# Turning the x operands of two token blocks by transposing DMAs instead of TensorE transposes and ScalarE copies

## The chip, the core and the metric

The kernel runs on one core of one Trainium2 chip. The metric is the device time of one execution in microseconds. The engines are TensorE (PE; its weight loads are PEld), VectorE (DVE), ScalarE (ACT), GpSimd (POOL) and SyncE (SP), whose queue issues most DMAs, in order; all DMAs run on 16 DMA engines.

## What is computed

`u` has 2048 tokens of 512 features. It is normalised (`xn`), and three terms are summed: `u` itself, a long convolution with a state-space kernel, and a mixture of eight experts in which all eight are used (top 8 of 8), so each token goes through every expert:

```
xn = layernorm(u)
out = u + s4_conv(xn) + xn * Dskip + sum_e gate[:, e] * (silu(xn @ w1[e]) @ w2[e])
# w1: 8 x 512 x 1792, w2: 8 x 1792 x 512, gate = softmax(xn @ w_gate)
```

The kernel keeps float32 accuracy with float16 matmuls: each operand is split into a high and a low half, and a product is three matmuls (high x high, high x low, low x high).

## The kernel before, in words

The experts run one after another (loop `e`), each over four blocks of 512 tokens (loop `tb`). The first product of an expert, `xn @ w1`, is done by a seven-product scheme on 2x2 blocks (Strassen-Winograd): instead of four quarters of x it takes seven sums and differences of them. For a token block `g` these operands are needed with features on partitions, in high and low halves. They lie in DRAM in `xd[g]` and are loaded from there into the single SBUF tile `xop`, seven pieces of 256 KB, at the end of the block before (lines 1562 to 1566, in `block`): each piece as soon as the last product that reads the old piece has been issued.

The operands are made once, while the first expert runs. Block 0 is handled by a separate path. Block 1 is turned straight into `xop`. Blocks 2 and 3 are made for `xd` in halves `(g, a)`, by these steps:

- `x_sums` (line 230): VectorE forms the seven sums, and SP stores the plain x to DRAM (lines 246 to 248, tensor `xnd`).
- `x_high` (line 251): ScalarE casts them to the high half, tile `xh`, one buffer. `x_low` (line 257): VectorE makes the low half, tile `xl`, one buffer.
- `x_turn` (line 264), four times for a half, `q` = 0 to 3 (0 and 1 the high half, 2 and 3 the low one): eight or six TensorE transposes of 128x128 into the shared PSUM bank `tp`, a ScalarE copy to the tile `xs` in SBUF (line 287), and two DMAs by SP to `xd` (line 291).

The order of all work is written out by hand. Time is counted in slots; 16 slots make a token block, four of them (one call of `block`) a group of expert columns. In a slot the products of `xn @ w1` are issued first, with ScalarE's work on them (`activate`, line 1355, which writes the tiles `ahl`); then the functions put into `mid`; then `pop` issues matmuls of the second product, which read `ahl` tiles of earlier slots; then the functions put into `side` and the pieces of work on the next expert's weights, which a planner admits by ScalarE time left (`act_room`, `work_on`). `early` stands before the products, `copied` behind the first of them. The registrations of the steps above are at lines 1466 to 1485: half `n` begins in slot `s0 = 20 + 4 n`, so the third block (`g` = 2, used from slot 32) is made in slots 20 to 27 and the fourth (used from slot 48) in slots 28 to 37.

The tiles `xs` and `ahl` share the nine buffers of the tag `hh`. The PSUM bank of `tp` is shared with other small products; `take_bank`, `bank_free` and the set `turns` keep their users apart: `turns` holds slots in which a step of the totals for a weight scale (`piece_end`, line 546) may not begin its bank use.

Of the kernel before, what the change touches and what calls it, by code (L numbers as in the profile page):

```python
# [10 lines left out]
F16 = mybir.dt.float16  # L11
# [7 lines left out]
P = 128  # L19
# [14 lines left out]
def s4_moe_kernel(  # L34
# [15 lines left out]
    nc = tc.nc  # L50
    V, S, T = nc.vector, nc.scalar, nc.tensor
# [17 lines left out]
    sb = ctx.enter_context(tc.tile_pool(name="sb", bufs=2))  # L69
# [13 lines left out]
    xop = cp.tile([P, 7, 2, 2, TH], F16, name="xop")  # L83
# [7 lines left out]
    xd = [dr.tile([P, 7, 2, 2, TH], F16, name=f"xd{g}") for g in range(NB)]  # L91
# [9 lines left out]
    clock = {"slot": 0, "pe": 0.0, "pe0": 0.0, "dve": 0.0, "dve0": 0.0, "left": 0.0,  # L101
             "act": 0.0, "act0": 0.0, "pe1": 0.0, "actleft": 0.0, "two": False}
    bank = {"out": None, "at": -1}

    def take_bank(out=None):

        f, bank["out"] = bank["out"], None
        if f:
            f()
            bank["at"] = clock["slot"]  # L110
        bank["out"] = out

    def bank_free():


        if bank["out"]:
            if clock["two"]:
                return False
            take_bank()
        return clock["slot"] > bank["at"]  # L120
# [104 lines left out]
    xs_ = {}  # L225
# [4 lines left out]
    def x_sums(g, a):  # L230


        ut, rs8 = uts[g], xs_["rs8", g]
        i0, i1 = g * TPB + a, g * TPB + a + 2
        m0, m1, r0, r1 = mean[:, i0:i0 + 1], mean[:, i1:i1 + 1], rs8[:, a:a + 1], rs8[:, a + 2:a + 3]
        fa_ = sb.tile([P, 4, TH], F32, tag="k4", name=f"xfa{g}_{a}", bufs=1)
        fb_ = sb.tile([P, 3, TH], F32, tag="v3", name=f"xfb{g}_{a}", bufs=1)
        a21 = sb.tile([P, TH], F32, tag="z", name=f"a21{g}_{a}", bufs=1)
        V.tensor_scalar(fa_[:, 0:2, :].rearrange("p a d -> p (a d)"), ut[a], m0, r0, op0=ALU.subtract, op1=ALU.mult)
        V.tensor_scalar(a21, ut[a + 2][:, 0:TH], m1, r1, op0=ALU.subtract, op1=ALU.mult)  # L240
        V.tensor_scalar(fa_[:, 2, :], ut[a + 2][:, TH:], m1, r1, op0=ALU.subtract, op1=ALU.mult)
        V.tensor_tensor(fa_[:, 3, :], a21, fa_[:, 2, :], op=ALU.add)
        V.tensor_tensor(fb_[:, 0, :], fa_[:, 3, :], fa_[:, 0, :], op=ALU.subtract)
        V.tensor_tensor(fb_[:, 1, :], a21, fa_[:, 0, :], op=ALU.subtract)
        V.tensor_tensor(fb_[:, 2, :], fa_[:, 1, :], fb_[:, 0, :], op=ALU.subtract)
        nc.sync.dma_start(xnd[:, i0, :], fa_[:, 0:2, :].rearrange("p a d -> p (a d)"))
        nc.sync.dma_start(xnd[:, i1, 0:TH], a21)
        nc.sync.dma_start(xnd[:, i1, TH:], fa_[:, 2, :])
        xs_["f"] = ((fa_, 0, 4), (fb_, 4, 3))

    def x_high(g, a):
        hi = xs_["hi"] = sb.tile([P, 7, TH], F16, tag="ta", name=f"xh{g}_{a}", bufs=1)
        for src, n0, n in xs_["f"]:
            S.copy(hi[:, n0:n0 + n, :].rearrange("p o d -> p (o d)"), src.rearrange("p o d -> p (o d)"))
            clock["act"] += at_(n * TH)

    def x_low(g, a):
        hi = xs_["hi"]
        lo = xs_["lo"] = sb.tile([P, 7, TH], F16, tag="tt", name=f"xl{g}_{a}", bufs=1)
        for src, n0, n in xs_["f"]:  # L260
            V.tensor_tensor(lo[:, n0:n0 + n, :].rearrange("p o d -> p (o d)"), src.rearrange("p o d -> p (o d)"),
                            hi[:, n0:n0 + n, :].rearrange("p o d -> p (o d)"), op=ALU.subtract)

    def x_turn(g, a, q):


        hi, lo = xs_["hi"], xs_["lo"]
        if g == 1:
            parts = [(r // 4, r // 2 % 2, r % 2) for r in range(8 * q, min(8 * q + 8, 28))]
        else:  # L270
            b, o0 = q // 2, q % 2 * 4
            no = min(4, 7 - o0)
            parts = [(o0 + r // 2, b, r % 2) for r in range(2 * no)]
        n = len(parts)
        take_bank()
        tp = ps_s.tile([P, 8, P], F16, tag="s4", name=f"tp{g}_{a}_{q}")
        for r, (o, b, k) in enumerate(parts):
            T.transpose(tp[:, r, :], (hi, lo)[b][:, o, k * P:(k + 1) * P], ident)  # L278
        if g == 1:
            dst = xop.rearrange("p o a k t -> p (o a k) t")[:, 8 * q:8 * q + n, a * P:(a + 1) * P]  # L280
            if q % 2:
                V.tensor_copy(dst, tp[:, :n, :])
            else:
                S.copy(dst, tp[:, :n, :])
        else:
            xs = sb.tile([P, 4, 2, P], F16, tag="hh", name=f"xs{g}_{a}_{q}", bufs=9)
            S.copy(xs.rearrange("p o k t -> p (o k) t")[:, :n], tp[:, :n, :])
            clock["act"] += at_(n * P)
            bank["at"] = now()
            for k in range(2):  # L290
                nc.sync.dma_start(xd[g][:, o0:o0 + no, b, k, a * P:(a + 1) * P], xs[:, :no, k])

    def x0_send(n):

# [10 lines left out]
    def x0_load():  # L305
        xs_["x0"] = sb.tile([P, 2, KT, TB], F16, tag="tb", name="x0", bufs=1)
        nc.sync.dma_start(xs_["x0"], x0d)
# [141 lines left out]
    def prepass_end(e, w, n):  # L449
        r = sb.tile([P, 1], F32, tag="r2", name=f"r2_{e}_{w}")  # L450
        V.tensor_reduce(r, rows[e, w][:, :n], axis=AX.X, op=ALU.add)
        yield
        st = pow2_total(r, 1, f"w{e}_{w}")
        yield
        if bank["out"]:
            take_bank()
        if w == 0:
            sc = scales[e] = sb.tile([P, 5], F32, tag="sc", name=f"sc{e}", bufs=2)
            w1_scales(sc, st, f"w{e}")
        else:  # L460
            sc = scales[e]
            pow2_scale(sc[:, 1:2], st, f"v{e}")
            pow2_inverse(sc[:, 4:5], sc[:, 1:2])
            V.scalar_tensor_tensor(sc[:, 4:5], sc[:, 4:5], float(2.0 ** (XSH - 1 + ASH)), sc[:, 2:3], op0=ALU.mult, op1=ALU.mult)
            ge_ = sb.tile([P, NT], F32, tag="gse", name=f"gse{e}", bufs=2)
            gates_e[e] = ge_
            if e > 1:
                V.tensor_scalar(ge_, gate[:, :, e], sc[:, 4:5], None, op0=ALU.mult)
# [77 lines left out]
    def piece_end(e, w, n, ready):  # L546

        st = {"g": prepass_end(e, w, n)}

        def step(k):  # L550
            st["at"] = now()
            next(st["g"], None)
            done.add((e, w, k))
            clock["dve"] += (0.2, 0.0, 0.9)[k]

        def can_go():
            if "at" not in st:
                return ready()
            return now() > st["at"] + 1 and bank_free() and now() + 1 not in turns
        it = Item(None, [lambda raw, k=k: step(k) for k in range(3)], can_go)  # L560
        it.e, it.w, it.sums = e, w, False
        return [it]
# [349 lines left out]
    def at_(n):  # L912

        return n / 1050 + 0.17
# [10 lines left out]
    def now():  # L925
        return clock["slot"]
# [174 lines left out]
    for pr in range(3, NPR):  # L1101
        for h in range(2):
            n = 2 * (pr - 3) + h
            tag, bufs = ("sE", 1) if n == 0 else ("sCB", 3) if n < 4 else ("stg", 4)
            t = sb.tile([P, D], F32, tag=tag, name=f"f0_{pr}_{h}", bufs=bufs)
# [9 lines left out]
    for pr in range(NPR):  # L1115
        t = w2s[pr].rearrange("p a f d -> p (a f d)").bitcast(F32)
# [289 lines left out]
        lows.append((first_split(2), True, False, None))  # L1406
    early, mid, copied = {}, {}, {}

    turns = set()

    def at(n, f, where=side):
        where.setdefault((0, n // 16, n % 16 // 4, n % 4), []).append(f)
    for n in range(7):
# [53 lines left out]
    for n, (g, a) in enumerate(halves):  # L1467
        s0 = 20 + 4 * n
        at(s0, lambda g=g, a=a: x_high(g, a), copied if n == 0 else side)
        at(s0 + 1, lambda g=g, a=a: x_low(g, a))  # L1470
        for q in range(4):
            n1, where = s0 + 2 + q, mid
            if (g, a) == (2, 1):
                n1, where = ((26, early), (26, mid), (27, early), (27, mid))[q]
            elif (g, a) == (2, 0) and q > 1:
                n1, where = 24, (early, mid)[q - 2]
            at(n1, lambda g=g, a=a, q=q: x_turn(g, a, q), where)
            turns.add(n1 - 2)
        if a == 0:
            at(s0 + 3, lambda g=g: x_sums(g, 1))  # L1480
            at(s0 + 3, lambda g=g: load_x(g + 1) if g + 1 < NB else x0_load())
        elif g + 1 < NB:
            at(s0 + 1, lambda g=g: norm_sums(g + 1))
            at(s0 + 2, lambda g=g: x_stats(g + 1))
            at(s0 + 3, lambda g=g: x_sums(g + 1, 0))
# [42 lines left out]
    for i in range(NT):  # L1528
        n = (i + 2) // 3
# [184 lines left out]
```

## Time and profile before

| what | value |
| --- | --- |
| timed runs (3) | 2329.56, 2329.60, 2330.28 us; median 2329.6 |
| span of the profiled execution | 2329.1 us |
| TensorE busy | 2315.5 us, 99% of the span |
| VectorE, ScalarE, GpSimd busy | 84%, 63%, 15% of the span |
| granted TensorE clock | 1.000 over the span |
| DMA | 320.72 MB in 327686 packets, 138 GB/s on average |

The span runs from the first to the last instruction of one execution; no other time of that execution is given, and the median of the timed runs is 0.5 us longer. In the rows below, `x8` behind a row is a count of instructions that the view has merged, `SPq` is an issue on SP's queue, and "to landing" runs from the issue of a DMA to its completion.

### The profile page before, as it was taken

To read this page: it belongs to the slowest core of one execution; us is meant where nothing else is said; L and a number is where in the kernel's file an instruction comes from. 1 tells how busy PE (TensorE), PEld (TensorE's weight loads), DVE (VectorE), ACT (ScalarE), POOL (GpSimd) and SP (SyncE) were. 2 spreads that over 40 slices of the span, in tenths; PEclk is the share of its full clock that TensorE was granted. 3 is DMA by queue.
4 is the path that set the end of the run, shared out by engine and by line. 5 is a ranking of instruction groups with operands and counts; after the bars stand their busy time and mean duration, and the time that the engine had idled before them with its cause. 6 is when DMAs were issued, how large, how long until landed. Compare 5 with 4: busy or idle time off the path is not lost.

```text
span 2329.1 us, 45278 instructions
## 1 busy us (share of the span) xinstructions
PE 2315.5 (99%) x17713; PEld 1540.1 (66%) x17713; DVE 1964.7 (84%) x3816; ACT 1466.2 (63%) x2585; POOL 339.7 (15%) x394
## 2 busy tenths in 40 slices
PE   8999999999999999999999999999999999999999
PEld 4666666666666666666666666666666666666665
DVE  8864877999999999999899989999989987997721
ACT  7676666657666576665766657666566665764543
POOL 0000011121111211111111111111111110111112
PEclk9999999999999999999999999999999999999999
DMA  8597456665566755655556545565465663643447
GB/s 281 181 264 199 111 137 151 146 146 118 133 160 144 149 129 130 155 117 107 131 121 161 117 102 139 125 148 123 99 144 123 145 133 86 154 94 65 81 87 176
DMA packets 327686, 320.72 MB, mean 138 GB/s; under 512 B 183664, under 2 KB 220016, under 8 KB 327024
## 3 DMA queue, kind: packets, MB, share of 16 engines
q1 hardware_dynamic: 271024, 223.70, 32.5%
q0 software_dynamic: 55872, 93.61, 25.5%
q8 instruction: 138, 2.26, 0.4%
q14 instruction: 76, 0.62, 0.1%
q10 hardware_dynamic: 576, 0.52, 0.1%
HBM read 202.14 MB, written 66.06 MB: 115 GB/s over the span
## 4 chain that ended last, share of the span: by engine, by line
PE 98%; ACT 1%; DVE 1%; DMA 0%; issue 0%; SPq 0%; DVEq 0%; ACTq 0%
PE hb L1348 43%; PE y L1333 16%; PE y L1331 16%; PE y L1332 16%; PE hb L1623 2%; PE kgen L769 1%; PE yp L900 1%; PE kf L840 1%; PE uf L827 1%; PE tp L278 0%; DMA xop<-xd 0%; DMA ut0b<-in_u_dram 0%; DMA kd<-ksb 0%; ACT ahl L1368 0%; ACT ye L1306 0%
## 5 line engine op out<-in xcount | busy, mean ns | idle before, releaser
L1348 PE MATMUL hb<-xop,w1s 128*128 128x256 f16 x9114 | 1072.6, 273 | 0.7 <-ACT scC L1570 0.4
L1348 PEld LDWEIGHTS <-w1s 128*128 128x128 f16 x9114 | 885.2, 98 | 174.1 <-issue 1.9
L1333 PE MATMUL y<-w2s,ahl 128*128 128x512 f16 x1792 | 679.2, 379 | 0.0
L1332 PE MATMUL y<-w2s,ahl 128*128 128x512 f16 x1792 | 679.2, 379 | 0.0
L1331 PE MATMUL y<-w2s,ahl 128*128 128x512 f16 x1792 | 679.2, 379 | 0.0
L1333 PEld LDWEIGHTS <-ahl 128*128 128x128 f16 x1792 | 175.4, 98 | 211.4
L1541 POOL DMA_DIRECT2D scC<-sE x124 | 120.3, 970 | 1282.9 <-ACT sE L1570 1050.6
L1364 ACT ACTIVATE fa<-hb,sc 128x512 f32<-128x512 f32 (+1 forms) x252 | 160.6, 637 | 200.5 <-PE hb L1348 196.6
L872 DVE TENSOR_TENSOR s<-s,tm 128x720 f32<-128x720 f32 (+14 forms) x480 | 268.9, 560 | 16.6
L1332 PEld LDWEIGHTS <-ahl 128*128 128x128 f16 x1792 | 175.4, 98 | 161.3
L1331 PEld LDWEIGHTS <-ahl 128*128 128x128 f16 x1792 | 175.4, 98 | 161.1
L871 DVE TENSOR_TENSOR tm<-v,k 128x720 f32<-128x720 f32 (+14 forms) x480 | 267.4, 557 | 10.6
L1377 DVE SCALAR_TENSOR_TENSOR ahl<-fa,sc,ahl 128x512 f16<-128x512 f32 (+1 forms) x262 | 178.6, 682 | 60.9 <-ACT ahl L1368 60.4
L1585 ACT COPY hb<-hb 128x512 f32<-128x512 f32 x124 | 64.1, 517 | 231.9 <-PE hb L1348 231.7
L1368 ACT ACTIVATE ahl<-fa,sc 128x512 f16<-128x512 f32 (+1 forms) x262 | 175.8, 672 | 8.5
L1541 POOL DMA_DIRECT2D scB<-sE x124 | 107.0, 863 | 428.9 <-ACT scB L1570 291.9
L1575 ACT COPY hb<-hb 128x512 f32<-128x512 f32 x124 | 64.3, 519 | 164.0 <-PE hb L1348 163.4
L1377 DVE SCALAR_TENSOR_TENSOR ahl<-scB,sc,ahl 128x512 f16<-128x512 f32 x124 | 84.4, 680 | 78.6 <-ACT ahl L1368 76.3
L757 DVE TENSOR_TENSOR tb<-ta,tt 128x64 f32<-128x64 f32 (+2 forms) x192 | 131.9, 687 | 5.6
L751 DVE TENSOR_TENSOR ta<-tb,zr 128x64 f32<-128x64 f32 (+2 forms) x192 | 131.6, 685 | 5.2
L1377 DVE SCALAR_TENSOR_TENSOR ahl<-scC,sc,ahl 128x512 f16<-128x512 f32 x124 | 84.2, 679 | 59.7 <-ACT ahl L1368 55.0
L1309 POOL DMA_DIRECT2D oacc<-ye x108 | 96.2, 1343 | 248.1 <-ACT ye L1306 246.4
(247 smaller groups left out, 2451.0 us busy)
## 6 DMA issues: line engine op xcount, KB each, us to landing
xop<-xd SPq DMA_DIRECT2D x210, 256.0 KB, 3.9
pp<-in_w_dram SPq DMA_DIRECT2D x98, 512.0 KB, 4.0
raw<-in_w_dram SPq DMA_DIRECT2D x56, 512.0 KB, 5.4
oacc<-ye POOLq DMA_DIRECT2D x108, 256.0 KB, 6.4
scC<-sE POOLq DMA_DIRECT2D x93, 256.0 KB, 4.2
scB<-sE POOLq DMA_DIRECT2D x93, 256.0 KB, 4.1
raw<-in_w_dram SPq DMA_DIRECT2D x52, 256.0 KB, 4.0
raw<-in_w_dram SPq DMA_DIRECT2D x104, 128.0 KB, 4.0
```

The source lines that it names most:

```text
L751: V.tensor_tensor(ta, tin, zrv, op=ALU.mult)
L757: V.tensor_tensor(tout, ta, tt, op=ALU.add)
L871: V.tensor_tensor(tm, v3f[:, :, 0:n], kb, op=ALU.mult)
L872: V.tensor_tensor(s3[:, :, m:], s3[:, :, m:], tm, op=ALU.add)
L1331: T.matmul(y, lhs[0], w2s[pr][:, 0, fh, :], start=(c == 0), stop=False)
L1332: T.matmul(y, lhs[0], w2s[pr][:, 1, fh, :], start=False, stop=False)
L1333: T.matmul(y, lhs[1], w2s[pr][:, 0, fh, :], start=False, stop=(c == NF - 1))
L1348: T.matmul(dst[:, q, :], w1s[pr][:, a, wo, k * P:(k + 1) * P], xop[:, xo, b, k, :], start=(first_mm and q == 0 and n == 0), stop=(n == 5), ...
L1364: S.activation(fa, src[:, :n], AF.Silu, scale=w1_unscale(e, d if whole else prs[0]))
L1368: S.activation(ahl[:, 0, :n], fa, AF.Copy, scale=scales[e][:, 3:4])
L1377: V.scalar_tensor_tensor(ahl[:, 1, :n], fa, sc[:, 3:4], ahl[:, 0, :n], op0=ALU.mult, op1=ALU.subtract)
L1541: nc.gpsimd.dma_start(dst, src, accum_op=ALU.add)
```

## The change

For blocks 2 and 3 `x_turn` no longer uses TensorE, the PSUM bank and ScalarE: one DMA transpose, issued by SP, reads the high or low half in SBUF and writes the turned tile `xs` in SBUF. The two sends to `xd` become a function of their own, `x_sent`, that is called a slot later, in `side` position. The registrations change: `q` = 0, 1 are turned in the slot after `x_high`, `q` = 2, 3 in the next, two in a slot, all in `mid` position; the set `turns` is gone. Block 1 is turned on TensorE as before.

```diff
@@ x_turn
+        if g > 1:
+            xs = xs_["t", q] = sb.tile([P, 4, 2, P], F16, tag="hh", name=f"xs{g}_{a}_{q}", bufs=9)
+            nc.sync.dma_start_transpose(xs.rearrange("p o k t -> p (o k) t")[:, :2 * no],
+                                        (hi, lo)[b][:, o0:o0 + no, :].rearrange("p o d -> p (o d)"))
+            return
...
-            xs = sb.tile([P, 4, 2, P], F16, tag="hh", name=f"xs{g}_{a}_{q}", bufs=9)
-            S.copy(xs.rearrange("p o k t -> p (o k) t")[:, :n], tp[:, :n, :])
-            clock["act"] += at_(n * P)
-            bank["at"] = now()
-            for k in range(2):
-                nc.sync.dma_start(xd[g][:, o0:o0 + no, b, k, a * P:(a + 1) * P], xs[:, :no, k])
+    def x_sent(g, a, q):
...
+        for k in range(2):
+            nc.sync.dma_start(xd[g][:, o0:o0 + no, b, k, a * P:(a + 1) * P], xs_["t", q][:, :no, k])
@@ piece_end
-            return now() > st["at"] + 1 and bank_free() and now() + 1 not in turns
+            return now() > st["at"] + 1 and bank_free()
@@ registrations
         for q in range(4):
-            n1, where = s0 + 2 + q, mid
-            if (g, a) == (2, 1):
-                n1, where = ((26, early), (26, mid), (27, early), (27, mid))[q]
-            elif (g, a) == (2, 0) and q > 1:
-                n1, where = 24, (early, mid)[q - 2]
-            at(n1, lambda g=g, a=a, q=q: x_turn(g, a, q), where)
-            turns.add(n1 - 2)
+            at(s0 + 1 + q // 2, lambda g=g, a=a, q=q: x_turn(g, a, q), mid)
+            at(s0 + 2 + q // 2, lambda g=g, a=a, q=q: x_sent(g, a, q))
```

## Rows read from the trace of the kernel before

**Rows 1.** The page's first part: busy time, share of the span and instructions of each engine.

```profile
PE 2315.5 (99%) x17713; PEld 1540.1 (66%) x17713; DVE 1964.7 (84%) x3816; ACT 1466.2 (63%) x2585; POOL 339.7 (15%) x394
```

**Rows 2.** The chain of work that ended last: shares of the span by engine.

```profile
PE 98%; ACT 1%; DVE 1%; DMA 0%; issue 0%; SPq 0%; DVEq 0%; ACTq 0%
```

**Rows 3.** What TensorE's matmuls waited for in the whole run: microseconds in total, times, longest.

```profile
PE tp L353 <- ACT xhl L343: 6.7, 1, 6.7
...
PE hb L1348 <- DMA xop<-xd: 0.3, 1, 0.3
```

**Rows 4.** Busy time of each engine from 115 to 163 us, with counts, granted clock, DMA share and GB/s. Columns: stretch, its length, PE, PEld, DVE, ACT, POOL.

```profile
115.00:163.00 48.00, 48.00 (x395) 32.82 (x393) 33.22 (x85) 38.19 (x62) 4.35 (x5) 1.00 1.02 284
```

**Rows 5.** The tile `tp` from 100 to 200 us: the transposes of blocks 2 and 3 and the copies out of it, with duration in ns (min/median/max), first and last start in us.

```profile
L278 PE MATMUL tp<-ident,xh x56: 219/219/219, 111.8 to 173.5; 128*128 128x128 f16 x56
L278 PE MATMUL tp<-ident,xl x56: 219/219/219, 119.1 to 180.8; 128*128 128x128 f16 x56
L287 ACT COPY xs<-tp x16: 778/897/1039, 113.1 to 183.9; 128x1024 f16<-128x1024 f16 x8, 128x768 f16<-128x768 f16 x8
```

**Rows 6.** TensorE in order of time around two turns: start, length, line, operation.

```profile
119.09 0.61 PE L278 MATMUL tp<-ident,xl 128*128 128x128 f16 x8
119.54 1.47 PE L1348 MATMUL hb<-xop,w1s 128*128 128x256 f16 x12
120.85 0.50 PE L278 MATMUL tp<-ident,xl 128*128 128x128 f16 x6
121.19 0.38 PE L1331 MATMUL y<-w2s,ahl 128*128 128x512 f16 x1
```

**Rows 7.** ScalarE's groups of instructions by line and form from 100 to 200 us: the copies of the turned tiles. Columns: busy us, mean ns, idle before.

```profile
L287 ACT COPY xs<-tp 128x1024 f16<-128x1024 f16 x8 | 8.1, 1010 | 3.1 <-PE tp L278 3.1
...
L287 ACT COPY xs<-tp 128x768 f16<-128x768 f16 x8 | 6.4, 795 | 1.1 <-issue 1.1
```

**Rows 8.** The tile `xd`: how long SP is held by issuing one load of operands and one send of a turned tile, in ns (min/median/max), with first and last start in us.

```profile
L1566 SPq DMA_DIRECT2D xop<-xd x210: 319/369/3792, 144.3 to 2239.6; - x105
L291 SPq DMA_DIRECT2D xd<-xs x32: 359/482/1552, 114.2 to 185.1; - x32
```

**Rows 9.** DMA issues from 95 to 200 us: KB each, median us from issue to landing.

```profile
xd<-xs SPq DMA_DIRECT2D x16, 128.0 KB, 4.1
...
xop<-xd SPq DMA_DIRECT2D x7, 256.0 KB, 3.5
...
ut<-in_u_dram SPq DMA_DIRECT2D x4, 256.0 KB, 6.4
```

**Rows 10.** DMA issues of the whole run, the slowest of 256 KB.

```profile
tb<-in_u_dram SPq DMA_DIRECT2D x2, 256.0 KB, 10.2
```

**Rows 11.** SP's queue in order of time from 126 us, as the third block's operands are completed and first loaded: start, length of the issues together, line, operation, count.

```profile
126.68 0.43 SPq L1487 DMA_DIRECT2D xd<-xop  x1
...
129.95 0.72 SPq L1487 DMA_DIRECT2D xd<-xop  x1
130.71 0.92 SPq L474 DMA_DIRECT2D pp<-in_w_dram  x2
131.67 0.43 SPq L1487 DMA_DIRECT2D xd<-xop  x1
...
136.00 1.56 SPq L1487 DMA_DIRECT2D xd<-xop  x1
137.60 0.56 SPq L474 DMA_DIRECT2D pp<-in_w_dram  x1
...
142.66 0.47 SPq L246 DMA_DIRECT2D xnd<-xfa  x1
143.23 0.39 SPq L247 DMA_DIRECT2D xnd<-a  x1
143.71 0.40 SPq L248 DMA_DIRECT2D xnd<-xfa  x1
144.29 3.97 SPq L1566 DMA_DIRECT2D xop<-xd  x5
```

**Rows 12.** VectorE in order of time: the end of the low half of the third block's second half, and of the fourth block's first.

```profile
130.27 0.95 DVE L261 TENSOR_TENSOR xl<-xfb,xh 128x768 f16<-128x768 f32 x1
...
146.56 0.95 DVE L261 TENSOR_TENSOR xl<-xfb,xh 128x768 f16<-128x768 f32 x1
```

**Rows 13.** TensorE in order of time: the first products of the third block's first, second and fourth slot.

```profile
152.43 1.47 PE L1348 MATMUL hb<-xop,w1s 128*128 128x256 f16 x12
...
158.07 2.78 PE L1348 MATMUL hb<-xop,w1s 128*128 128x256 f16 x24
...
170.57 2.78 PE L1348 MATMUL hb<-xop,w1s 128*128 128x256 f16 x24
```

**Rows 14.** ScalarE in order of time at the change from the second to the third block; in brackets, idle time before and what ended it.

```profile
150.85 0.51 ACT L1368 ACTIVATE ahl<-fa,sc 128x256 f16<-128x256 f32 x1
151.27 0.35 ACT L1570 COPY scB<-hb 128x256 f32<-128x256 f32 x1
...
153.99 0.57 ACT L1575 COPY hb<-hb 128x512 f32<-128x512 f32 x1 [1.67 <-PE hb L1348]
```

More of the change, by code (lines that the diff above doesn't have):

```diff
@@ L272, in x_turn @@
             no = min(4, 7 - o0)
-            parts = [(o0 + r // 2, b, r % 2) for r in range(2 * no)]
+        if g > 1:
[3 more added lines that the diff above has]
+            return
         n = len(parts)
@@ L278, in x_turn @@
             T.transpose(tp[:, r, :], (hi, lo)[b][:, o, k * P:(k + 1) * P], ident)
[L279 to L284, printed above, removed]
-        else:
-            xs = sb.tile([P, 4, 2, P], F16, tag="hh", name=f"xs{g}_{a}_{q}", bufs=9)
-            S.copy(xs.rearrange("p o k t -> p (o k) t")[:, :n], tp[:, :n, :])
-            clock["act"] += at_(n * P)
-            bank["at"] = now()
-            for k in range(2):
-                nc.sync.dma_start(xd[g][:, o0:o0 + no, b, k, a * P:(a + 1) * P], xs[:, :no, k])
+        dst = xop.rearrange("p o a k t -> p (o a k) t")[:, 8 * q:8 * q + n, a * P:(a + 1) * P]
+        if q % 2:
+            V.tensor_copy(dst, tp[:, :n, :])
+        else:
+            S.copy(dst, tp[:, :n, :])
+    def x_sent(g, a, q):
+        b, o0 = q // 2, q % 2 * 4
+        no = min(4, 7 - o0)
+        for k in range(2):
+            nc.sync.dma_start(xd[g][:, o0:o0 + no, b, k, a * P:(a + 1) * P], xs_["t", q][:, :no, k])
     def x0_send(n):
@@ L1407, in s4_moe_kernel @@
     early, mid, copied = {}, {}, {}
-    turns = set()
     def at(n, f, where=side):
```

## The prediction

> **What bounds the kernel now.** I read the page's first part, then the chain of waits, then what TensorE itself waited for. TensorE is busy for 2315.5 of the 2329.1 us span [rows 1], the chain that ends last is 98% TensorE [rows 2], and of its few idle microseconds the longest wait, 6.7 us, lies at the start; the only wait for a transfer of x operands in the whole run is 0.3 us [rows 3]. So time is won by taking work off TensorE's stream and lost by anything that makes it wait. The change acts on the stretch from about 106 to 186 us. In the middle of it, from 115 to 163 us, TensorE is busy for all 48 us at full clock, ScalarE for 38 and VectorE for 33, and the DMA engines are as good as full, with a share of 1.02 [rows 4]. ScalarE time given back is therefore worth nothing by itself; TensorE time is worth its full length; and new transfers go where transfers already queue.
>
> **What it removes.** 112 transposes of 128x128 [rows 5] and the 16 ScalarE copies out of PSUM. What a transpose costs is not its printed length of 219 ns, which is a latency: they are pipelined. The cost is from start to next start. A turn of eight starts at 119.09 and the matmul behind it at 119.54, a turn of six takes 120.85 to 121.19 [rows 6]: 0.45 and 0.34 us, or 56 ns each. Eight turns of each kind give 8 x 0.45 + 8 x 0.34 = 6.3 us; 112 x 56 ns is 6.3 as well, and I take 6.2, since stamps of some other turns read 0.44 and 0.33. All of it lies on the path. The Trainium skill ("TensorE: Matmul & The Clock Gate", Part 4: PE-mode transpose) speaks of about 275 ns for a transpose in a kernel; by that the gain would be 30.8 us. The timeline contradicts it here, since the next instruction's start does not wait that long.
>
> The 16 copies are 8 x 1.010 + 8 x 0.795 = 14.4 us of ScalarE [rows 7]. They go at no direct gain, for TensorE hid them. One PSUM bank is also taken 16 times less, and the rule that kept the steps of the scale totals off the turns goes: nothing of TensorE waits for either in rows 3, so zero. The planner books some ScalarE time less and may start squares or splits of the next expert a slot earlier in the third block; TensorE runs on through them now, so zero too.
>
> **What it adds.** Sixteen transposing DMAs on SP's queue, of 256 or 192 KB, two in a slot, and the sends of a pair moved behind them by a slot, in side position. The 32 sends stay. The trace shows no transposing DMA, so I bound it. Call h the time by which one of them holds back what stands behind it on SP. The nearest row is the issue of a send of the same tile: 0.36 to 1.55 us, 0.48 in the middle [rows 8]. The far end is that SP is held until the data has landed: 4.1 us as for a send, 6.4 as for a load of 256 KB in this full stretch [rows 9], 10.2 as for the slowest 256 KB load of the run [rows 10]. Below nothing it can't be, as an issue takes time. I take h = 0.5, since SP issues the next transfer 0.4 to 0.6 us after one that itself takes about 4 us to land: 142.66, 143.23, 143.71 [rows 11].
>
> What waits behind it matters most for the second half of the third block, whose data TensorE wants first. SP, in order: high pair, other issues, low pair, four high sends, four low sends (these wait for the landing), three stores of the plain x, then the five loads of the third block's operands, the first at 144.29 [rows 11]. High pair: SP is free for it at about 127.1, after the copy issued at 126.68. Low pair: VectorE has the low half at 130.27 + 0.95 = 131.2 [rows 12]. The other issues in between are 0.72 + 0.92 + 0.43 + 1.56 + 0.56 = 4.2 us, the sends 8 x 0.48 = 3.9, the stores 1.3 [rows 8, 11]: 9.3. The first load lands after 3.5 [rows 9], so at 127.1 + 4h + 9.3 + 3.5 = 139.9 + 4h. TensorE uses it at 152.43 [rows 13], less the ten turns that no longer stand before (5 x 0.78 = 3.9): 148.5. So the stall is 4h - 8.6, and **h up to 2.1 us costs nothing**. With h = 0.5 the load waits for VectorE's plain x as now, and lands near 146 to 148: covered, but with 1 to 2 us in hand and not the 4 of today.
>
> The last two loads stand behind both pairs of the next half and its four high sends: 5 x 0.37 + 4 x 0.48 = 3.8, and 4h [rows 8]. They are used at 170.57, 18.1 after 152.43 [rows 13], of which three more turns (1.2) go: a second stall of 3.8 + 4h - (18.1 - 1.2) = 4h - 13.1. Together 8h - 21.7.
>
> New waits elsewhere: the converted halves sit in one buffer each, so the next conversion waits until the transposing DMAs have read it; these come two slots or more (over 9 us) ahead of it, against a landing of 4 to 6. In the fourth block's operands nothing is urgent, as they are fetched ten slots later.
>
> **Sum.** -6.2 on TensorE, +0 for SP, +0 for ScalarE. Against the profiled span of 2329.1 that is 2322.9; the median of the runs is 2329.6, 0.5 above the span, so **2323.4**. That is 0.27%; about 0.2% (4.7 us) is what a measurement here tells from no change, so only 1.5 us may be lost for it still to read as faster.
>
> **Rival 1, slower: SP is held.** Place: SP between 127 and 150 us. Price: 8h - 21.7 of stall against 6.2. It passes +4.7 at h = 4.1, the landing of one send; with 6.4 the stalls are 29.5 and the time 2352.9, with 10.2 it is 2383. For it: the queue is in order, the DMA engines there are full, and a transfer that moves two-byte elements to other partitions may be no ordinary one. Against it: SP's issues last 0.3 to 0.6 us whatever the landing [rows 11]. I take 2353 as its time. The pages of the skill disagree on this. "VectorE: DVE Perf Modes", The three transpose paths, gives 1309 ns for one 128x128 on the DMA crossbar; seven in a row on average would be h = 9.2, and an estimated time of 2375. "Advanced Engine Details and Errata", X-Bar Transpose (TRN2), says transposing DMAs are as fast as regular ones, which is my forecast. No row here decides between them.
>
> **Rival 2, no change: a buffer in place of the bank.** The turned tiles share nine buffers with the activated tiles. By my count of the program's order, at the end of the second block six to seven activated tiles wait for their matmuls, while four turned tiles are now live from the issue to the landing of their sends, where one or two were. Then the activation that ends the block (150.85 now, about 147 after) must wait for the first high send: low half at 146.56 + 0.95 = 147.5 [rows 12], issues of 1 to 2, landing of 4.1 to 6.4, so about 153.5 to 156. After it ScalarE still has 0.51, 0.35 and the copy of 0.57 [rows 14], which TensorE needs for the second product of the next slot, at 158.07 + 1.3 less 4.4 = 155. It would come at about 155 to 157.5: 0 to 2.5 us lost, perhaps twice. Time 2323.4 + 1.5 to 5, say 2326. For it: tiles are short. Against: ScalarE idles before that copy now (1.67 us) and gets 14.4 us back.
>
> **Rival 3, the full DMA engines alone.** At share 1.02 the additional 3.7 MB (16 x 224 KB, as much as the 32 sends carry) push back other transfers by some microseconds: loads of the operands land after 6.4 in place of 3.5, and the margin of 1 to 2 us is gone; 1 to 2 us of stall, 2325. Its outcome falls on the border of faster and no change.
>
> **Chances.** Forecast 0.50; rival 2 0.20; rival 3 0.10, half of it still faster; rival 1 0.20. So faster 0.55, within 0.2% 0.25, slower 0.20. The likeliest case has its own range, 2322.4 to 2324.9. The range over all starts at 2322.4, the sum less 1 us for shifts in the plan, and goes to 2336: it takes in rivals 2 and 3 and the lower end of rival 1 (h = 4.1 to 4.3), and leaves out most of rival 1, under 2 in 10.
>
> **What would show it.** Right: 56 transposes on the same line in place of 168, TensorE's matmul stream without gaps between 100 and 190 us, the transposing DMAs' issues on SP under 1 us each, the first load of the third block's operands issued before 144 us, ScalarE busy about 14 us less. Wrong: TensorE waiting for that load at about 148 us (rival 1 or 3: the issue's length tells which), or an activation of ScalarE idle for a send at the end of the second block and a gap in TensorE some 5 us later (rival 2). A gain well above 6.2 us would mean that turns cost more than the stamps show.

## The result and the profile after

The changed kernel takes **2345.07 us** (median of six runs, 2334.27 to 2346.80) against 2329.69 for the kernel before on the same chip (six runs): ratio 1.0057, 95% interval 1.0041 to 1.0072. It is slower by 15.4 us, where 6.2 us of gain were forecast; 21.6 us have to be found. The profiled execution is the slowest of the six: 2346.8 us for a span of 2345.0. The time around the span is thus 1.8 us and not the 0.5 that the prediction inferred.

What was to go has gone. The page's first part, which answers to [rows 1]: TensorE has 112 instructions less, ScalarE 13.4 us less.

```profile
PE 2315.8 (99%) x17601; PEld 1535.7 (65%) x17601; DVE 1964.7 (84%) x3816; ACT 1452.8 (62%) x2569; POOL 339.2 (14%) x394
```

TensorE's busy time has not fallen although 112 transposes are gone, and the next view says why. Busy time by stretch (columns as in [rows 4]), first of the kernel before:

```profile
97.00:215.00 118.00, 118.00 (x931) 81.53 (x930) 68.99 (x156) 90.47 (x145) 12.27 (x14) 1.00 0.78 217
```

and of the changed kernel:

```profile
97.00:215.00 118.00, 102.34 (x703) 66.10 (x701) 63.52 (x133) 69.13 (x116) 10.49 (x12) 0.93 1.00 237
...
139.00:145.00 6.00, 5.01 (x33) 3.04 (x31) 4.67 (x16) 0.36 (x1) 0.00 (x0) 1.00 1.18 68
145.00:151.00 6.00, 0.00 (x0) 0.00 (x0) 0.75 (x1) 2.28 (x3) 0.00 (x0) 0.68 1.29 161
151.00:157.00 6.00, 4.85 (x18) 2.69 (x18) 3.24 (x4) 3.87 (x9) 0.37 (x1) 0.50 1.15 284
...
175.00:181.00 6.00, 4.42 (x26) 3.22 (x26) 1.89 (x4) 5.55 (x12) 0.00 (x0) 0.74 1.00 333
```

Read the last two columns of 139 to 145 first: the DMA engines are busier than full, at a share of 1.18, and move 68 GB/s, a quarter of the 284 in [rows 4]; the text below calls this the crawl. TensorE then stands still from 144 to 152 us, and the granted clock is 0.50 from 151 to 157, its lower level of 1.2 GHz. From 97 to 215 us TensorE idles 15.7 us where it idled none before, and its busy time there is swollen by the clock: 4.85 us at 0.50 and 4.42 at 0.74 alone are some 3.6 us of work lost (an estimate: busy time times the missing share of the clock). Idle and slow time together outweigh the 6.2 us saved.

What TensorE and ScalarE waited for from 95 to 215 us (total, times, longest):

```profile
ACT ahl L1371 <- PE y L1336: 10.4, 2, 7.1
...
PE hb L1351 <- ACT hb L1581: 8.5, 2, 8.1
ACT scC L1367 <- DMA scC<-sE: 8.1, 1, 8.1
...
ACT ahl L1371 <- DMA xd<-xs: 6.6, 3, 4.3
...
PE hb L1351 <- DMA xnd<-xfa: 2.8, 1, 2.8
...
PE hb L1351 <- DMA xop<-xd: 1.5, 1, 1.5
```

The 8.1 us of TensorE hang on the 8.1 us of ScalarE. The 2.8 us put down to a store (`xnd`) end with a late copy of ScalarE (175.96, 0.57 us long; TensorE goes on at 176.59), which stands behind the 4.3 us wait for a send. The chain can be followed in three timelines. SP's queue, the part that answers to [rows 11]:

```profile
133.58 4.77 SPq L275 DMA_TRANSPOSE xs<-xh  x2
138.41 3.37 SPq L1483 DMA_DIRECT2D xd<-xop  x1
141.87 7.60 SPq L275 DMA_TRANSPOSE xs<-xl  x2
149.56 2.73 SPq L294 DMA_DIRECT2D xd<-xs  x4
...
158.15 1.47 SPq L1562 DMA_DIRECT2D xop<-xd  x3
```

GpSimd's queue issues the DMAs that add a partial sum `sE` onto `scC` or `scB`, SBUF to SBUF. This is line 1537, unchanged in text, a bystander of the change:

```profile
113.71 0.86 POOL L1537 DMA_DIRECT2D scC<-sE  x1 [11.48 <-ACT sE L1566]
...
133.85 0.86 POOL L1537 DMA_DIRECT2D scC<-sE  x1 [15.99 <-ACT sE L1566]
```

ScalarE, two instructions with the idle time before them:

```profile
148.69 0.72 ACT L1367 ACTIVATE scC<-scC,sc 128x512 f32<-128x512 f32 x1 [8.13 <-DMA scC<-sE]
...
171.79 0.51 ACT L1371 ACTIVATE ahl<-scC,sc 128x256 f16<-128x256 f32 x1 [4.25 <-DMA xd<-xs]
```

And TensorE:

```profile
152.15 2.72 PE L1351 MATMUL hb<-xop,w1s 128*128 128x256 f16 x12 [8.14 <-ACT hb L1581]
```

A pair of transposing DMAs (the two of the high half, the high pair) is issued at 133.58, an accumulating DMA at 133.85. The sum lands at 148.7, 14.8 us later. ScalarE's activation waits for it, the copies behind that activation come late, and with them TensorE's next product, whose twelve matmuls last 2.72 us at the lower clock where the same twelve took 1.47 [rows 13]. The high pair is as late, after 15.0 and 14.4 us. Issues and landings, first two from 133 to 134.5 us, then the medians from 95 to 200 us:

```profile
scC<-sE POOLq DMA_DIRECT2D x1, 256.0 KB, 14.8
xs<-xh SPq DMA_TRANSPOSE x1, 15.0
...
scC<-sE POOLq DMA_DIRECT2D x4, 256.0 KB, 5.5
xs<-xh SPq DMA_TRANSPOSE x8, 4.8
xs<-xl SPq DMA_TRANSPOSE x8, 4.7
```

and of the kernel before, for the same sums:

```profile
scC<-sE POOLq DMA_DIRECT2D x5, 256.0 KB, 3.5
```

The sum and the pair are not alone: a plain store of SP in the same stretch (`xd<-xop`, 138.41) landed after 12.7 us. How long SP was held, from the tile `xs`:

```profile
L294 SPq DMA_DIRECT2D xd<-xs x32: 433/543/1504, 116.1 to 192.5; - x32
L275 SPq DMA_TRANSPOSE xs<-xh x8: 1243/1573/3386, 108.3 to 179.9; - x8
L275 SPq DMA_TRANSPOSE xs<-xl x8: 1222/1498/6276, 112.9 to 184.7; - x8
```

A transposing DMA holds SP for 1.5 us (median) where the send next to it takes 0.54. Its landing, 4.8 and 4.7 us in the median, is hardly later than that of a send of half the size (4.1 in [rows 9]). The Trainium skill ("Advanced Engine Details and Errata", X-Bar Transpose (TRN2)) calls transposing DMAs as fast as regular ones: the landing agrees, the issue does not.

### The profile page after: what moved, and what is told of

It is laid out like the page before. It is cut to its first block, busy times and chain, and to the rows that moved or that the text cites. A ratio compares the mean times of both kernels' runs of the same rounds, so it can differ in the third digit from the quotient of the medians.

```text
span 2345.0 us, 45055 instructions
## 1 busy us (share of the span) xinstructions
PE 2315.8 (99%) x17601; PEld 1535.7 (65%) x17601; DVE 1964.7 (84%) x3816; ACT 1452.8 (62%) x2569; POOL 339.2 (14%) x394
## 2 busy tenths in 40 slices
DMA packets 342533, 324.37 MB, mean 138 GB/s; under 512 B 198512, under 2 KB 234864, under 8 KB 341872
## 4 chain that ended last, share of the span: by engine, by line
PE 96%; DMA 2%; ACT 1%; SPq 1%; DVE 0%; issue 0%; DVEq 0%; ACTq 0%
PE hb L1351 42%; PE y L1335 16%; PE y L1334 16%; PE y L1336 16%; PE hb L1619 2%; PE kgen L772 1%; PE uf L830 1%; PE kf L843 1%; PE yp L903 1%; DMA scC<-sE 1%; DMA xd<-xs 0%; SPq L294 0%; DMA scB<-sE 0%; DMA raw<-in_w_dram 0%; ACT ahl L1371 0%
```

## The experiments

Four readings stood after the two traces. **Two kinds of DMA:** transposing DMAs and GpSimd's accumulating ones, in flight together, hold each other up. **Buffers** (rival 2): activations wait for a tile of the nine. **SP** (rival 1): the transposing DMAs delay what is queued behind them. **Bytes** (rival 3): any further 3.7 MB would do the same. Unless another is named, a kernel is the changed one with the edit shown; every ratio is to the kernel before on the same chip, with its 95% interval. Differences between two kernels are those of their medians. The runs come from several chips, on which the kernel before took 2329.69 to 2330.17 us, and those against the changed kernel are the least sharp, since its interval reaches from 9.6 to 16.8 us over the kernel before.

**Own buffers.** Twelve of the sixteen turned tiles leave the shared nine.

```diff
-            xs = ... tag="hh", name=f"xs{g}_{a}_{q}", bufs=9)
+            tag, bufs = ("hh", 9) if (g, a) == (2, 0) else ("stg", 4)
+            xs = ... tag=tag, name=f"xs{g}_{a}_{q}", bufs=bufs)
```

> The changed kernel, but twelve of the sixteen turned tiles (all but those of the third block's first half) lie in the four buffers of the staging tiles, which nothing else uses in those slots, so that activations no longer wait for a buffer held by a turned tile. Theory A (the transposing DMAs and GpSimd's accumulating DMAs, in flight together, hold each other up; ScalarE waits 8.1 us for scC and TensorE behind it, and the granted clock falls after it): the wait of 8 us at about 145 us stays, and only the later stalls (ScalarE's 10.4 us behind TensorE, 6.6 us behind sends, about 5 us of TensorE) go; 2336 to 2342. Theory B (the nine shared buffers are the cause): nearly all stalls go, 2324 to 2328. Theory C (SP is held by the issue of the transposing DMAs and everything behind is late): no change, 2340 to 2346.

Measured: 2341.71 us (four runs, 2338.34 to 2342.84), 1.0049 [1.0034, 1.0064]. Two rows of its windows and waits:

```profile
139.00:145.00 6.00, 4.05 (x26) 2.32 (x24) 5.51 (x19) 1.80 (x3) 0.00 (x0) 1.00 1.48 110
```

```profile
PE hb L1352 <- ACT hb L1582: 6.8, 1, 6.8
```

The activations no longer wait for the second product's matmuls, but the DMA engines still crawl and TensorE still waits 6.8 us in one piece. The staging buffers are not quite free, though: ScalarE's copy to `ye` waits 3.0 us for one until a send has landed. Buffers are not the main cause: the two medians are 3.4 us apart, less than either kernel scatters.

**No accumulating DMAs.** In slots 20 to 38 GpSimd adds in SBUF.

```diff
-        nc.gpsimd.dma_start(dst, src, accum_op=ALU.add)
+        if 20 <= now() <= 38:
+            nc.gpsimd.tensor_tensor(dst, dst, src, op=ALU.add)
+        else:
+            nc.gpsimd.dma_start(dst, src, accum_op=ALU.add)
```

> The changed kernel, but in slots 20 to 38 the sums scC + sE and scB + sE are computed by GpSimd in SBUF instead of by GpSimd's accumulating DMAs. Theory A: with no accumulating DMA beside them the transposing DMAs land after about 4 to 5 us everywhere and hold SP under 2 us each, the 8 us wait at 145 us is gone; what stays are the buffer waits, 2328 to 2334. Theory B: same stalls as before, 2338 to 2346. Theory C: SP held as before at 134 and 142 us (4.8 and 7.6 us for a pair), 2338 to 2346.

Measured: 2330.03 us (ten runs, 2327.49 to 2333.80), 1.0003 [0.9994, 1.0013]: **15.0 us faster than the changed kernel**, with all sixteen transposing DMAs kept. The profiled execution is the fastest of the ten (2327.49). Its stretch and what TensorE still waited for:

```profile
139.00:145.00 6.00, 5.56 (x39) 3.60 (x37) 5.78 (x11) 5.60 (x11) 0.00 (x0) 1.00 1.08 282
```

```profile
PE hb L1351 <- ACT hb L1584: 2.7, 2, 2.3
PE hb L1351 <- DMA xop<-xd: 0.6, 1, 0.6
```

282 GB/s in place of 68 from 139 to 145 us. The control, the kernel **before** with the same edit:

> The kernel before with only the sums of slots 20 to 38 by GpSimd in SBUF: the control. If the accumulating DMAs cost something in the kernel before as well, it gains; theory A says that they do harm only beside transposing DMAs: 2328.5 to 2331, no change.

Measured: 2329.93 us (ten runs), 1.0000 [0.9991, 1.0009]. The additions are worth nothing by themselves; they matter only beside transposing DMAs.

**Plain copies.** The same bytes from the same tiles to the same tiles, not turned.

```diff
-            nc.sync.dma_start_transpose(xs..., (hi, lo)[b]...)
+            nc.sync.dma_start(xs..., (hi, lo)[b]...)
```

> The changed kernel with a plain DMA copy from SBUF to SBUF of the same bytes in place of each transposing DMA (the turned tiles hold x not turned, so the numbers that come out are others); order, waits and sends are unchanged. If it is the transposing that jams the engines (theory A), the copies land after about 4 us, SP is held 0.5 us by each, no 8 us wait: 2325 to 2331, the rest being buffer waits. If it is only that more bytes go through full DMA engines, the time stays at 2338 to 2346. Theory B: the buffer waits stay as they are, 2336 to 2346.

Measured: 2332.38 us (ten runs, 2330.99 to 2333.76), 1.0011 [1.0001, 1.0020]. With the accumulating DMAs beside them:

```profile
139.00:145.00 6.00, 4.89 (x32) 2.99 (x31) 3.60 (x10) 1.08 (x2) 0.00 (x0) 1.00 1.10 270
```

```profile
L275 SPq DMA_DIRECT2D xs<-xh x8: 471/572/740, 108.6 to 166.3; - x8
```

No crawl, and an issue of 0.5 us. Bytes are not what costs 15 us. But this kernel has no transposes on TensorE either, and still loses the whole 6.2 us and 2.4 more. In its profile the longest stop of TensorE stands behind a wait for a shared buffer, as in rival 2, with the granted clock at 0.75 from 145 to 151 us behind it; what the added bytes and issues cost beside it was not separated.

```profile
ACT ahl L1371 <- DMA xd<-xs: 3.2, 1, 3.2
...
PE hb L1351 <- ACT hb L1581: 4.0, 1, 4.0
```

**Plain copies on GpSimd's queue instead of sums.**

```diff
+        if 20 <= now() <= 38:
+            nc.gpsimd.dma_start(dst, src)
+        else:
...
```

> The changed kernel with GpSimd's DMAs of slots 20 to 38 as plain copies of the same bytes from sE to scC and scB, without adding (so the numbers that come out are others); their places and waits are unchanged. Theory A1 (it is the accumulating that cannot go beside a transpose): 2328 to 2334, as with the sums off the DMA. Theory A2 (any traffic of GpSimd's software queue beside a transposing DMA jams): 2338 to 2346, with landings of over 10 us for scC near 134 us.

Measured: 2336.28 us (ten runs, 2333.85 to 2340.76), 1.0027 [1.0018, 1.0036]. Its window and its low pair on SP:

```profile
139.00:145.00 6.00, 4.26 (x28) 2.53 (x26) 3.54 (x9) 1.83 (x4) 0.00 (x0) 1.00 1.27 151
```

```profile
137.13 7.45 SPq L275 DMA_TRANSPOSE xs<-xl  x2
```

In between: 8.8 us faster than with sums, 6.3 slower than without those DMAs. So adding onto the destination makes it worse, but a transfer of GpSimd's queue need not add to disturb a transposing one.

**The suspected cost by itself.** The kernel before, all its work kept, with the transposing DMAs as additional transfers that nothing reads. A first form gave all of them one buffer:

```diff
...
+        t = sb.tile([P, 8, P], F16, tag="zi", name=f"xx{g}_{a}_{q}", bufs=1)
+        nc.sync.dma_start_transpose(t[:, :2 * no], (hi, lo)[b]...)
...
+            at(s0 + 1 + q // 2, lambda g=g, a=a, q=q: x_extra(g, a, q), mid)
```

> The kernel before, whole, with the sixteen transposing DMAs added at the places where the changed kernel has them; they write one scratch tile that nothing reads. TensorE transposes, copies and buffers are as before. It prices the transposing DMAs by themselves: theory A says that they hold up other transfers (an accumulating DMA beside them lands after over 10 us) and TensorE is stopped although nothing reads what they write: 2333 to 2345. Theory B says that without the shared buffers they cost next to nothing, 2329 to 2331. Theory C: SP's queue is held and the operands' loads are late, 2335 to 2345, with the waits on xop and not on scC.

Measured: 2358.30 us (four runs), 1.0118 [1.0101, 1.0135]. This tells nothing apart: each transfer waits on SP for the landing of the one before. The second form has a buffer for each of a pair (only the first of the low pair takes that of the first of the high pair), and a twin with GpSimd's adds:

```diff
...
+        t = sb.tile([P, 2 * no, P], F16, tag=("zi", "b1", "zi", "b2")[q], ...)
...
```

> The kernel before, all its work kept, with the sixteen transposing DMAs added at the slots of the changed kernel. They write scratch tiles that nothing reads, each of its own buffer within a pair; only the first tile of the low pair takes the buffer of the first of the high pair, a slot later. GpSimd's accumulating DMAs stay. Theory that transposing DMAs and GpSimd's accumulating DMAs hold each other up: 8 us or more over the kernel before (2338 or more), a stretch near 133 to 150 us in which the DMA engines move under 170 GB/s at a share over 1, and an accumulating DMA that lands after 10 us or more. Theory that only bytes and SP's time count: 2 to 5 us over, the same as its twin with GpSimd's adds.

> The same with the additions of slots 20 to 38 done by GpSimd on SBUF instead of accumulating DMAs. Theory of the two kinds of DMA: most of the excess goes; what is left is SP held for 16 x 1.5 = 24 us in a full queue, 1 to 5 us (2331 to 2335). Theory of bytes and SP's time: as its twin.

Measured: with accumulating DMAs 2341.90 us (five runs, 2339.41 to 2346.31), 1.0050 [1.0036, 1.0064]; with GpSimd's adds 2332.47 us (eleven runs, 2329.87 to 2335.32), 1.0011 [1.0003, 1.0020]. The stretch of the first (its profiled execution is the slowest of the five, 2346.31), and the landing of its sums onto `scC`:

```profile
139.00:145.00 6.00, 6.00 (x39) 3.62 (x37) 3.32 (x8) 1.75 (x4) 0.86 (x1) 1.00 1.37 123
145.00:151.00 6.00, 1.10 (x6) 0.41 (x5) 1.07 (x2) 3.00 (x6) 0.00 (x0) 0.88 1.16 244
...
DMA to landing us min/median/max: 3.5/6.0/11.0
```

What ScalarE and TensorE waited for in it:

```profile
ACT ahl L1375 <- DMA xd<-xs: 7.5, 2, 4.5
...
PE hb L1355 <- ACT hb L1593: 4.9, 1, 4.9
```

The same stretches of the second:

```profile
139.00:145.00 6.00, 6.00 (x41) 3.67 (x39) 5.52 (x14) 3.35 (x7) 1.27 (x1) 1.00 1.08 233
145.00:151.00 6.00, 5.79 (x47) 3.94 (x46) 4.60 (x7) 5.70 (x12) 0.76 (x1) 1.00 1.02 289
```

Nothing reads what these sixteen transfers write, and yet they cost 11.7 us beside the sums and 2.3 without. The meeting of the two kinds of DMA is worth 9.4 us in a kernel that is otherwise the one before. The path to TensorE is another than in the changed kernel: ScalarE waits 1.6 us for the late sum and longer for late sends, whose tiles share buffers with its own.

**What is left without it.** Both first edits together, own buffers and GpSimd's adds:

> The changed kernel with both remedies: turned tiles of the last three halves in buffers of their own, and the sums of slots 20 to 38 by GpSimd in SBUF. Theory A plus B (the jam of transposing and accumulating DMAs cost about 15 us, the shared buffers most of the 6 to 7 us that were still missing): TensorE without gaps, 2323.5 to 2326, faster than before by 0.15 to 0.27%. If the buffers are not what was left (SP's hold of 1.25 to 1.5 us for each transposing DMA and late loads of operands are): 2328 to 2331, like the run with the sums alone.

Measured: 2329.73 us (eleven runs, 2327.53 to 2331.12), 0.9997 [0.9988, 1.0006]. The activations wait for no buffer any more and nothing is won by it over the adds alone (0.3 us), since the next wait is that of rival 1, at the place where the prediction put it:

```profile
129.72 3.37 SPq L276 DMA_TRANSPOSE xs<-xh  x2
...
134.96 3.96 SPq L276 DMA_TRANSPOSE xs<-xl  x2
...
147.15 1.27 SPq L1566 DMA_DIRECT2D xop<-xd  x3
```

```profile
150.55 1.87 PE L1352 MATMUL hb<-xop,w1s 128*128 128x256 f16 x12 [2.43 <-DMA xop<-xd]
```

The operands of the third block's first product come 2.4 us late. To take away just that, the half that TensorE wants first, `(2, 1)`, goes back to TensorE as in the kernel before, at 28 of the 112 transposes, with the slots kept free for it:

```diff
...
-        if g > 1:
+        if g > 1 and (g, a) != (2, 1):
...
+            if (g, a) == (2, 1):
+                n1, where = ((26, early), (26, mid), (27, early), (27, mid))[q]
+                at(n1, lambda g=g, a=a, q=q: x_turn(g, a, q), where)
+                continue
```

Alone, with shared buffers and accumulating DMAs:

> The changed kernel with one of its four halves, the third block's second, turned on TensorE again as before (four turns, four ScalarE copies, their old places); the other three by transposing DMAs, with GpSimd's accumulating DMAs and the shared buffers. Turns saved: 12 of 16, 4.7 us. The jam of 133 to 149 us stood where this half's two pairs met the sums of GpSimd. Theory A says that it goes with them: 2327 to 2333, what is lost being buffer waits in the third block. If each pair jams wherever it stands, the others do so as well: 2336 or more. Theory C, with SP late for the operands' first load: that load comes before 145 us again, and no wait on xop.

Measured: 2336.78 us (ten runs, 2334.70 to 2338.32), 1.0027 [1.0018, 1.0037]. That is more than the 2327 to 2333 expected if the stop went with this half. The next half's pair, issued at 149.43 beside a sum of 149.08, is no crawl: the two land after 7.1 and 6.4 us, the sum after 4.7. But SP's queue is late by then, and ScalarE waits for a shared tile until a send behind that pair has landed:

```profile
161.38 0.51 ACT L1380 ACTIVATE ahl<-fa,sc 128x256 f16<-128x256 f32 x1 [11.46 <-DMA xd<-xs]
```

With the adds by GpSimd (below) the same pair goes out at 143.36 and the wait is 7.5 us. Where the 6 us on SP come from was not found; the sum issued at 132.91 landed after 9.0 us though the transposing DMAs before it had been issued by 115.5.

With both edits of before, then with the adds alone:

> The same with both remedies: buffers of their own for the fourth block's turned tiles and the sums of slots 20 to 38 by GpSimd in SBUF. No jam, no buffer wait, the first load of operands in time: 2329.9 less 4.7 and plus up to 1 us of small waits, 2325 to 2326.5. If it stays at 2329 to 2330, something is left that neither the jam, the buffers nor the late load explains.

> The same with the sums by GpSimd alone, and the shared buffers left as they are: it prices the buffers without the jam. Theory B: activations wait for turned tiles and for TensorE in the third block, 2 to 4 us slower than with buffers of their own, 2327.5 to 2330. If the buffers cost nothing, 2325 to 2326.5.

Measured: with both **2325.34 us** (eleven runs, 2324.63 to 2326.08), 0.9980 [0.9972, 0.9989], faster than either kernel; with the adds but shared buffers 2328.18 us (ten runs), 0.9992 [0.9983, 1.0001]. The first, its stretch and the issue of its first loads of operands:

```profile
97.00:215.00 118.00, 118.00 (x881) 80.06 (x879) 75.02 (x161) 87.68 (x147) 15.06 (x14) 1.00 0.91 245
```

```profile
142.20 1.28 SPq L1579 DMA_DIRECT2D xop<-xd  x3
```

TensorE has no gap left. Where the buffers are shared, in the second kernel, they cost 2.8 us, and by the rows that rival 2 had named: an activation that waits for a send, and a copy of ScalarE that TensorE waits for behind it.

```profile
ACT ahl L1380 <- DMA xd<-xs: 7.5, 1, 7.5
...
PE hb L1360 <- ACT hb L1587: 3.0, 2, 2.3
```

## Why the prediction was wrong

**What it removes: right.** 56 transposes remain of 168. With 84 gone and nothing in the way, 84 x 56 ns = 4.7 us were due and 4.8 came (the interval reaches from 2.6 to 6.5 us). A transpose cost the distance of the starts and not the printed 219 ns. ScalarE's time came back and was worth nothing, as said.

**What it adds: the step that failed.** The term "+0 for SP" priced a transposing DMA by two things only, how long it holds SP and how soon it lands itself. What it does to other transfers in flight beside it was no term of the sum; rival 3 thought of crowding by bytes, and came to 1 to 2 us. That is the main part of the 21.6 us: the accumulating DMAs taken away gives back 15.0; the transposing DMAs laid into the kernel before cost 9.4 more beside sums than without; plain copies of the same bytes bring no crawl. The bystander stood on the page of the kernel before, among its DMA issues, on a queue that the prediction never names: `scC<-sE`, 256 KB, SBUF to SBUF by GpSimd, every 20 us or so (113.71 and 133.85 in the changed kernel).

**The hold h: inside the bounds, badly taken.** Its median is 1.5 us, three times the value taken, which was that of the nearest row for a plain transfer. The reason given, that SP's issues last 0.3 to 0.6 us whatever the landing, is not what the rows say: [rows 8] has sends of up to 1.55 us and loads of up to 3.79. Nor is h one number: the pair issued at 160.43 in the fastest kernel held SP for 6.1 us, with no accumulating DMA beside it. By the prediction's own point (2.1 us costs nothing) 1.5 would still have been free. It was not: without the meeting and without buffer waits the load came 2.4 us late. TensorE wanted it at 148.1, as forecast (148.5); the load was issued at 147.15, where the prediction's terms give 142.4 with h = 1.5. From 127 us on every term is a little longer in that kernel's queue: the two pairs 7.3 us in place of 6.0, the other issues 5.2 for 4.2, the sends 4.6 for 3.9, the stores 1.6 for 1.3, and the pauses between issues, no term of the sum, 1.4. The mechanism was right and the threshold too generous; and the granted clock of 0.72 from 151 to 157 us made the gap dearer than its length.

**Rival 1** was thus real in place and small in size, and in the changed kernel it was hidden by a worse wait: there the load costs 1.5 us, although it is issued 14 us later than before (158.15 against 144.29), since everything had slid by then. **Rival 2** was right in mechanism and price: 2.8 us measured between the two kernels with a half back, 1.5 to 5 forecast. Its times hold too: the waiting activation starts at 155.64 (153.5 to 156 forecast) and TensorE loses 2.3 us there (0 to 2.5). **Rival 3** as stated, crowding by bytes, is not what happened; but the plain copies, 2.4 us over the kernel before, show that added bytes, issues and shared buffers together were worth more than the transposes would have brought.

**The sum, with what was measured,** in the order of the experiments: -6.2 for the transposes; +15.0 for the meeting of the two kinds of DMA; +6.3 for the rest (2330.03 against 2329.97 - 6.2), of which the half that is wanted first, taken off the DMAs, and the buffers together give back all. That makes 15.1 of the 15.4 us; the rest is the difference between the chips. How the 6.3 divides depends on the order of the edits: own buffers bring 0.3 while the load is late, 2.8 once it isn't.

**Open.** Why only some meetings crawl: in the changed kernel the sum issued at 113.71 among the first pairs landed after 5.2 us, and the one at 181.61, between two pairs, after 5.9. What inside the DMA engines makes the transfers wait for each other, and how the cost divides between the adding and GpSimd's queue as such: plain transfers there had about 6 of the 15 us. Whether it is the turning or the small packets: the transposing DMAs raise the packets under 512 B from 183664 to 198512, the plain copies of the same bytes to 183920, and no run moved these bytes in small packets without turning them. Why the changed kernel scatters over 12 us from run to run. Issuing the transposing DMAs from another queue was not tried.

## What to carry to other kernels

When a change adds a kind of transfer that the trace does not show, list every queue that is busy in its stretch, not only the one that it joins, and bound what it may do to the transfers beside it. A stretch with a high DMA share and few GB/s was the sign here that transfers disturbed each other; a control that puts the new transfer into the old kernel, unread, prices that alone. And a saved microsecond on the bounding engine is kept only if every operand still comes in time: here, with the sums and the buffers out of the way, one of four halves left where it was made the difference between nothing and 4.8 us.

## What the hardware did that was not expected

A transposing DMA and an accumulating DMA of GpSimd, both SBUF to SBUF, landed after 15.0 and 14.8 us when issued within 0.3 us of each other, against medians of 4.8 and 5.5 in the same kernel, while the DMA engines showed a share of 1.18 and moved 68 GB/s. The Trainium skill ("DMA: Bandwidth & Descriptors", Rules for kernel authors) says that "A transpose next to ordinary DMAs needs nothing". That is a rule on what must wait for what; as to time the runs differ from it where the neighbour is one of GpSimd's, by 9.4 us between the two kernels with unread transfers.

The issue of a transposing DMA held SP for 1.5 us in the median (1.2 at least), and a pair for up to 7.6 us in the crawl; a plain copy of the same tile took 0.5. A long hold alone is no sign of the crawl: in the five kernels with transposing DMAs and GpSimd's adds, no accumulating DMA beside them, the high pair of the last half held SP for 4.7 to 6.1 us, while the DMA engines moved 285 to 337 GB/s.

An idle time of 8 us was followed by a stretch at the lower clock, 0.50 granted from 151 to 157 us; the wait of 6.25 us in the kernel with one half back was followed by 0.55 from 163 to 169, one of 2.4 us (own buffers and adds) by 0.72 from 151 to 157. After 2.3 us of waiting in the kernel with the adds alone the clock stayed at 1.00. A wait that is followed by the lower clock costs more than its length.
